# Threshold attention followed by a feed-forward block: another spacing of the weight conversion, the diagonals and the last tile

## Chip, core and metric

One core of a Trainium2 chip runs the whole program. The metric is the device time of one execution in microseconds (us). The kernel before takes 1440.85 us (median of three runs, 1439.65 to 1445.99). The profiled execution has a span of 1438.9 us from its first to its last instruction.

## The reference, cut to what matters

For 8 sequences of 576 tokens and 8 heads of 64 features:

```python
scores = (q @ k.T) / 8
thresh = max(scores, axis=-1) - tau
scores = where(scores >= thresh, scores, -1e9)
attn   = exp(scores - max(scores)); attn = attn / sum(attn)
x      = heads side by side of (attn @ v)            # 8 x 576 x 512
xn     = (x - mean(x)) / sqrt(var(x) + 1e-6) * g_ln
out    = x + relu(xn @ w_ch1) @ w_ch2                # 512 -> 2048 -> 512
```

Everything is float32, but the two weight matrices arrive as float64 and are turned into float32 on the chip, by integer operations on their words.

## The kernel before, in words

**Slots.** Attention runs in 72 slots, nine for each sequence: four pairs of heads times two halves of the queries, and one slot (the fifth) for the last 64 queries of all four pairs. Each slot has on TensorE (PE) the scores (`scores`, L384), then on VectorE (DVE) the row maxima (`neg`, L398), on ScalarE (ACT) the exponentials (L409), and on VectorE again the threshold with the row sums (`weights`, L416, and the reciprocal, L420). The scores of a slot go into the PSUM banks of the slot before, so they wait for that slot's L416. Then the weights have to be turned. In the first nine slots TensorE does it: `turn_weights` multiplies each of four blocks by a diagonal matrix that holds 1/sum (`diag`, made by ScalarE from the identity, L427), into a PSUM tile `tp`, which ScalarE copies to `em` (L462); a fifth tile `tr` takes the rest. From slot 9 on GpSimd (POOL) divides (L429), VectorE transposes blocks of 32 (L494), and the result goes by DMA to DRAM (`scr`, L500) and back (`em`, L509). A slot later TensorE multiplies by the values (`values_of`, L538).

**Feed-forward groups.** There are 16 groups of 288 tokens. For each, TensorE forms the mean (`mean_of`), VectorE subtracts it (`centre`, `xc`, L579), and `ffn_steps` issues 16 first products of four (`p1`, L100, then ReLU by ScalarE, L649) and four second products of sixteen (`p2`, L100). After the second `p1`, ScalarE squares `xc` (L653) and GpSimd adds the squares (L655); at the ninth, TensorE forms the variance (`var`), and VectorE takes the inverse root (`root`, L620 to L628) in three portions. Each finished `p2` is multiplied by that root (`add_to_x`, L596, VectorE), added to x (L597, GpSimd), transposed (L602, VectorE) and sent out (L609, four DMAs). Mean, `tp`, `tr`, `p1`, `var` and `p2` share the two PSUM buffers of the tag "ff": a tile can only begin when the operation that empties one of the two has been done.

**What sets the order.** It is written by hand, with no scheduler. A slot has four quarters; the main loop at the end of the function calls `scores`, `exponentials`, `weights` and so on, and between them `second_part(n, i)` issues as many feed-forward products as a budget gives: the products that are left of a group, spread over the quarters up to `ready(g + 1)`, with the shares `ROOM`. The call `at_quarter` puts work off to a quarter of the next slot, and the lists `aside` and `stores` hold work for the next gap. Every engine works off its instructions in the order of these calls.

**Weight conversion.** The class `Weights` converts 32 chunks (16 of each matrix) of 128 x 512. `fetch` issues the DMA of a raw chunk into a free piece of memory (rooms that belong to tiles which are not in use yet: `w2_sb`, `hidden`, `et`, `x_room`, `stage`); the table in `__init__` says up to which chunk each room may be used. A `tick` moves up to four chunks by a step each: `begin` (VectorE L263 and L267, ScalarE L271 and L275), `carry` (GpSimd L281), `mask` (VectorE L290, three ticks later) and, for the first matrix only, `end` (ScalarE L303). Slots 0 to 2 have two ticks, slots 3 to 5 three, and all from slot 6 on six. A `p1` or `p2` is issued only when its chunks have been ended in the order of the calls.

Of the kernel before, what the change touches and what calls it, by code (L numbers as in the profile page):

```python
# [18 lines left out]
def kernel(  # L19
# [31 lines left out]
    nc = tc.nc  # L51
# [114 lines left out]
    class Weights:  # L166
# [13 lines left out]
        def __init__(self):  # L180
            self.chunks = [
                (w1_sb[i][:, c : c + WC], w_ch1[i * 128 : (i + 1) * 128, c : c + WC], i)
                for c in range(0, DF, WC)
                for i in range(NK)
            ] + [
                (
                    w2_sb[:, m, d : d + 4].rearrange("p d c -> p (d c)"),
                    w_ch2[d * 128 : (d + 4) * 128, m * 128 : (m + 1) * 128].rearrange(
                        "(d p) c -> p d c", p=128
                    ),  # L190
                    None,
                )
                for m in range(NK)
                for d in range(0, ND, 4)
            ]
            self.n1 = NK * (DF // WC)
            self.fetched = self.begun = self.carried = self.masked = self.ended = 0
            self.raw, self.made, self.due, self.ticks = {}, {}, [], 2
            flat = lambda t: t.rearrange("p a b -> p (a b)")

            x_room = ffn.tile([128, NK, TOK], F32, tag="x", bufs=3, name="x_room")
            stage = consts.tile([128, 8, WC], F32, name="stage")
            et = att.tile([128, NB, 128], F32, tag="et", bufs=1, name="et0")

            n1 = self.n1
            self.free = []
            for t, n, before in (  # L210
                (w2_sb.rearrange("p m d c -> p (m d) c"), ND // 2, lambda p: n1 + 2 * p),
                (hidden, 4, lambda p: 10),
                (et, 2, lambda p: 2 * n1),
                (x_room, 1, lambda p: 2 * n1),
                (stage, 4, lambda p: 2 * n1),
            ):
                for p in range(n):
                    self.free.append((before(p), -1, flat(t)[:, p * 2 * WC : (p + 1) * 2 * WC]))
# [192 lines left out]
    def weights(es, thr, divide):  # L411


        den = small.tile([128, 4], F32, tag="den", name="den")
        for i in range(4):
            nc.vector.scalar_tensor_tensor(  # L416
                out=es[:, i], in0=blocks[i], scalar=thr[:, i : i + 1], in1=es[:, i],
                op0=ALU.is_ge, op1=ALU.mult, accum_out=den[:, i : i + 1],
            )
        nc.vector.reciprocal(den, den)  # L420
        diags = []
        for i in range(4):
            if not divide:
                if i % 2 == 0:
                    two = ffn.tile([128, TOK], F32, tag="o", bufs=6, name="diag")
                diags.append(two[:, i % 2 * 128 : i % 2 * 128 + 128])
                nc.scalar.mul(diags[i], ident, den[:, i : i + 1])  # L427
                continue
            nc.gpsimd.tensor_scalar(  # L429
                out=es[:, i], in0=es[:, i], scalar1=den[:, i : i + 1], scalar2=1.0,  # L430
                op0=ALU.mult, op1=ALU.mult,
            )
        return diags


# [7 lines left out]
    def turn_weights(s, es, diags):  # L443


        em, er = turned_tiles(s)
        for i in range(4):
            if i == 2:
                yield
            tp = ps_ff.tile([128, J, 128], F32, tag="ff", name="tp")  # L450
            for c in range(J):
                product(
                    tp[:, c], lhsT=es[:, i, c * 128 : (c + 1) * 128], rhs=diags[i],
                    start=True, stop=True,
                )
            if s == HP:
                nc.scalar.copy(
                    em[:, :, :, 32 * i : 32 * i + 32], tp.rearrange("p c (a x) -> p c a x", a=4)
                )
            else:  # L460
                h, j = divmod(i, 2)
                nc.scalar.copy(  # L462
                    em[:, :, 2 * j : 2 * j + 2, 64 * h : 64 * h + 64],
                    tp.rearrange("p c (a x) -> p c a x", a=2),
                )
        tr = ps_ff.tile([64, 4, 128], F32, tag="ff", name="tr")
        for i in range(4):
            nc.tensor.matmul(  # L468
                tr[:, i], lhsT=es[:, i, J * 128 :], rhs=diags[i], start=True, stop=True
            )  # L470
        if s == HP:
            nc.scalar.copy(
                er[:64].rearrange("p a (u x) -> p u a x", u=HP),
                tr.rearrange("p u (a x) -> p u a x", a=4),
            )
        else:
            nc.scalar.copy(
                er[:64].rearrange("p a (h x) -> p h a x", h=2),
                tr.rearrange("p (h j) (a x) -> p h (j a) x", h=2, a=2),
            )  # L480
        yield em, er
# [106 lines left out]
    def run_all(calls):  # L588
        now = calls[:]
        calls.clear()  # L590
        for fn in now:
            fn()

    def add_to_x(g, m, p2, rb):
        o = ffn.tile([128, TOK], F32, tag="o", bufs=6, name="o")
        nc.vector.tensor_mul(o, p2, rb)  # L596
        nc.gpsimd.tensor_tensor(out=o, in0=o, in1=groups[g][:, m], op=ALU.add)  # L597
        aside.append(lambda: store(g, m, o))

    def store(g, m, o):  # L600
# [4 lines left out]
    def send(g, m, ot):  # L605
        b, t = divmod(g, 2)
        for i in range(4):
            f = m * 128 + 32 * i
            nc.sync.dma_start(  # L609
                out=out[b, t * TOK : (t + 1) * TOK, f : f + 32].rearrange(  # L610
                    "(n r) c -> r n c", r=32
                ),
                in_=ot[32 * i : 32 * i + 32].rearrange("p (n c) -> p n c", c=32),
            )
# [17 lines left out]
    def ffn_steps(g):  # L632
# [5 lines left out]
        for d in range(ND):  # L638
            while conversion.ended < 4 * (d // 4 + 1):
                yield 0  # L640
            p1 = ps_ff.tile([128, TOK], F32, tag="ff", name="p1")
            for c in range(NK):
                product(
                    p1, lhsT=w1_sb[c][:, d * 128 : (d + 1) * 128], rhs=xc[:, c],
                    start=(c == 0), stop=(c == NK - 1),
                )
                if c < NK - 1:
                    yield 1
            nc.scalar.activation(hidden[:, d], p1, func=AF.Relu)  # L649
            yield 2  # L650
            if d == 1:
                sq = ffn.tile([128, NK, TOK], F32, tag="sq", bufs=1, name="sq")
                nc.scalar.activation(sq, xc, func=AF.Square)  # L653
                for c in range(1, NK):
                    nc.gpsimd.tensor_tensor(out=sq[:, 0], in0=sq[:, 0], in1=sq[:, c], op=ALU.add)  # L655
            if d == 8:
                var = ps_ff.tile([128, TOK], F32, tag="ff", name="var")
                product(var, lhsT=avg_sb, rhs=sq[:, 0], start=True, stop=True)
                rb = ffn.tile([128, TOK], F32, tag="rb", bufs=2, name="rb")
                nc.scalar.activation(sq[:, 1], var, func=AF.Identity, bias=eps_sb)  # L660
                aside.append(lambda: root(rb, sq[:, 1], sq[:, 2]))
                yield 1
# [19 lines left out]
    ROOM = (0.6, 1.0, 1.25, 0.35)  # L682
    STEPS = 1 + NK * ND * 2
    queue = []
    issued = 0
    owed = 0.0
    later_calls = {}

# [7 lines left out]
    def ready(g):  # L696

        if g < 2:
            return (24, 42)[g]
        b, t = divmod(g, 2)  # L700
        return QUARTERS * (b * SLOTS + (HP, 2 * HP)[t] + 2) + (2, 4)[t]

    def second_part(n, i):

        nonlocal issued, owed
        if not queue:
            return
        at = QUARTERS * n + i
# [40 lines left out]
    load_v(1)  # L749
    for n in range(NS):  # L750
        b, s = divmod(n, SLOTS)
        ticks = (1, 3, 4)[: 2 + n // 3] if n < 6 else range(1, 7)

        def tick(i):
            if i in ticks:
# [20 lines left out]
        second_part(n, 1)  # L776
        tick(2)
        blocks_go = by_blocks(b * HP)
        diags = weights(es, thr, blocks_go)
        run_all(aside)  # L780
        run_all(stores)
        tick(3)
        run(n, 2)
        second_part(n, 2)
        tick(4)
        box = []
        if blocks_go:
            scr = turn_blocks(s, es)
            at_quarter(n + 1, 0, lambda s=s, scr=scr, box=box: box.append(fetch(s, scr)))
        else:  # L790
            made = turn_weights(s, es, diags)
            at_quarter(n + 1, -1, next, made)
            at_quarter(
                n + 1, 0 if s <= HP else -1, lambda made=made, box=box: box.append(next(made))
            )
        at_quarter(
            n + 1, 1 if b == 0 and s <= HP else 3,
            lambda b=b, s=s, box=box: values_of(b, s, box[0]),
# [51 lines left out]
```

## Time and profile before

| What | Value |
|---|---|
| Time, median of three | 1440.85 us |
| Span of the profiled execution | 1438.9 us |
| TensorE busy | 1389.7 us (97%) |
| VectorE busy | 870.5 us (60%) |
| ScalarE busy | 421.9 us (29%) |
| GpSimd busy | 439.5 us (31%) |
| All `p1` products (L100, p<-xc) | 517.5 us |
| All `p2` products (L100, p<-hidden) | 513.6 us |
| Mean granted clock of TensorE | 0.995 |

The share of busy time is a mean over the whole span. Seen in windows of 10 us it differs much: TensorE is busy for 8.4 of 10 us from 50 to 60 us and for 6.6 from 60 to 70, and from 240 to 420 us it has no gap to speak of. So what the change can do has to be read from the first 215 us and from the last few.

The slots of the first part can be told by the maxima of VectorE (L398), two operations for each slot. In the profiled execution those of slots 3 to 11 begin at 50.63, 65.17, 79.68, 93.11, 123.20, 149.08, 168.44, 194.94 and 215.39 us.

### The profile page before, as it was taken

How to read it: one execution, taken by the hardware profiler on the slowest of the kernel's cores; microseconds unless marked ns; L12 is line 12 of the kernel's file. 1: busy time of each engine (PE TensorE's matmuls, PEld its weight loads, DVE VectorE, ACT ScalarE, POOL GpSimd, SP SyncE). 2: the span in 40 equal slices, each digit the busy share in tenths (PEclk: the TensorE clock that was granted, in tenths of full speed). 3: DMA queues.
4: the chain of work that ended last, by engine and by line, in shares of the span. 5: the costliest groups of instructions: out<-in, count | busy, mean ns of one | idle time of the engine just before them, and what ended most of it. 6: DMA issues, size and time to landing. Idle time of an engine off the chain costs nothing.

```text
span 1438.9 us, 29660 instructions
## 1 busy us (share of the span) xinstructions
PE 1389.7 (97%) x12168; PEld 852.3 (59%) x12168; DVE 870.5 (60%) x1492; ACT 421.9 (29%) x818; POOL 439.5 (31%) x681
## 2 busy tenths in 40 slices
PE   4879999999999999999999999999999999999998
PEld 3655665655556555655556555665556555565664
DVE  5998857556665666556665565656665666656111
ACT  3886513132222313132221312213132222213020
POOL 2344342333323233232322233232332323222100
PEclk8999999999999999999999999999999999999999
DMA  9622456558855587557855577556775578455301
GB/s 226 173 70 82 90 130 164 163 136 172 178 145 144 142 182 169 143 134 170 188 152 145 147 151 175 142 145 146 173 177 146 131 170 185 135 145 136 79 6 17
DMA packets 466840, 205.12 MB, mean 143 GB/s; under 512 B 275024, under 2 KB 428368, under 8 KB 466704
## 3 DMA queue, kind: packets, MB, share of 16 engines
q1 hardware_dynamic: 461936, 202.64, 57.9%
q8 instruction: 95, 1.56, 0.5%
q10 hardware_dynamic: 4736, 0.59, 0.4%
q14 instruction: 41, 0.34, 0.1%
q0 software_dynamic: 32, 0.00, 0.0%
HBM read 119.41 MB, written 83.76 MB: 141 GB/s over the span
## 4 chain that ended last, share of the span: by engine, by line
PE 89%; DVE 4%; ACT 2%; SPq 1%; issue 1%; DMA 1%; POOL 0%; POOLq 0%; ACTq 0%; DVEq 0%
PE p L100 67%; PE sc L538 10%; PE sc L384 10%; PE tp L100 1%; DVE e L416 1%; DMA em<-scr 1%; DVE neg L398 1%; SPq L500 1%; PE mean L100 0%; PE var L100 0%; DVE w L263 0%; ACT e L409 0%; PE tr L468 0%; SPq L129 0%; SPq L133 0%
## 5 line engine op out<-in xcount | busy, mean ns | idle before, releaser
L100 PE MATMUL p<-xc,w 128*64 128x288 f32 x4096 | 517.5, 408 | 6.5 <-ACT hidden L649 4.5
L100 PE MATMUL p<-hidden,w 128*64 128x288 f32 x4096 | 513.6, 407 | 0.0
L100 PEld LDWEIGHTS p<-xc,w 128*64 128x64 f32 x4096 | 291.8, 137 | 216.3 <-ACT hidden L649 14.4
L100 PEld LDWEIGHTS p<-hidden,w 128*64 128x64 f32 x4096 | 295.3, 137 | 199.1 <-issue 9.3
L398 DVE TENSOR_REDUCE neg<-sc 128x2 f32<-128x1152 f32 x144 | 188.8, 1352 | 250.1 <-PE sc L384 250.1
L409 ACT ACTIVATE e<-sc,neg 128x576 f32<-128x576 f32 x288 | 194.4, 742 | 261.7 <-DVE neg L398 256.2
L429 POOL TENSOR_SCALAR e<-e,den 128x576 f32<-128x576 f32 x252 | 188.5, 766 | 240.5 <-DVE den L420 240.4
L416 DVE SCALAR_TENSOR_TENSOR e<-sc,thr,e 128x576 f32<-128x576 f32 x288 | 219.1, 811 | 27.8 <-ACT e L409 27.8
L494 DVE STREAM_TRANSPOSE et<-e 128x1152 f32<-128x1152 f32 x112 | 153.6, 1375 | 78.3 <-POOL e L429 58.2
L649 ACT ACTIVATE hidden<-p 128x288 f32<-128x288 f32 x256 | 105.7, 413 | 284.5 <-PE p L100 282.9
L384 PE MATMUL sc<-kT,qT 64*128 64x384 f32 (+3 forms) x1024 | 150.2, 424 | 20.0 <-DVE qT L344 10.1
L402 POOL TENSOR_SCALAR thr<-neg,low_sb 128x2 f32<-128x2 f32 x144 | 41.9, 291 | 352.2 <-DVE neg L398 343.3
L384 PEld LDWEIGHTS sc<-kT,qT 64*128 64x128 f32 x1024 | 94.2, 191 | 77.2 <-issue 27.5
L538 PE MATMUL sc<-em,v_in 128*64 128x256 f32 (+1 forms) x1408 | 131.4, 330 | 2.1 <-DMA em<-scr 2.1
L555 ACT COPY x<-sc 128x256 f32<-128x256 f32 x60 | 22.3, 372 | 316.9 <-PE sc L538 291.9
L538 PEld LDWEIGHTS sc<-em,v_in 128*64 128x64 f32 x1408 | 86.2, 138 | 41.6 <-issue 2.9
L597 POOL TENSOR_TENSOR o<-o,x 128x288 f32<-128x288 f32 x64 | 51.4, 804 | 151.4 <-DVE o L596 151.4
L596 DVE TENSOR_TENSOR o<-p,rb 128x288 f32<-128x288 f32 x64 | 28.1, 439 | 103.5 <-PE p L100 103.0
L564 POOL TENSOR_TENSOR sum<-sum,x 128x256 f32<-128x256 f32 (+1 forms) x64 | 32.7, 511 | 71.8 <-ACT x L555 69.3
L655 POOL TENSOR_TENSOR sq<-sq 128x288 f32<-128x288 f32 x48 | 38.8, 808 | 42.1 <-ACT sq L653 39.6
L564 POOL TENSOR_TENSOR sum<-x 128x256 f32<-128x256 f32 (+1 forms) x32 | 16.7, 523 | 98.8 <-ACT x L555 57.3
L538 PE MATMUL sc<-rest,v_rest 128*64 128x256 f32 (+1 forms) x352 | 44.4, 329 | 0.0
(130 smaller groups left out, 715.0 us busy)
## 6 DMA issues: line engine op xcount, KB each, us to landing
scr<-et SPq DMA_DIRECT2D x252, 288.0 KB, 4.8
em<-scr SPq DMA_DIRECT2D x63, 1024.0 KB, 5.9
out_dram<-ot SPq DMA_DIRECT2D x256, 36.0 KB, 4.2
q_in<-in_q_dram SPq DMA_DIRECT2D x124, 72.0 KB, 3.4
k_in<-in_k_dram SPq DMA_DIRECT2D x120, 72.0 KB, 2.6
v_in<-in_v_dram SPq DMA_DIRECT2D x64, 128.0 KB, 4.5
rest<-scr SPq DMA_DIRECT2D x63, 128.0 KB, 5.9
w<-in_moe_w_ch_dram SPq DMA_DIRECT2D x10, 512.0 KB, 5.9
```

What stands on the lines that cost most here:

```text
L100: nc.tensor.matmul(out[r], lhsT=lhsT[:, r], rhs=rhs, **flags)
L384: nc.tensor.matmul(sc[h][64 * i : 64 * i + 64 if s == HP else 128, at : at + n], lhsT=ql[r] if s == HP else qT[r, half, j * 128 : (j + 1) ...
L398: nc.vector.tensor_reduce(out=neg[:, i], in_=pairs[h], axis=AXL.X, op=ALU.max, negate=True,)
L402: nc.gpsimd.tensor_scalar(out=thr[:, i], in0=neg[:, i], scalar1=-1.0, scalar2=low_sb, op0=ALU.mult, op1=ALU.add,)
L409: nc.scalar.activation(es[:, i], blocks[i], func=AF.Exp, bias=neg[:, i : i + 1])
L416: nc.vector.scalar_tensor_tensor(out=es[:, i], in0=blocks[i], scalar=thr[:, i : i + 1], in1=es[:, i], op0=ALU.is_ge, op1=ALU.mult, accum_o ...
L429: nc.gpsimd.tensor_scalar(out=es[:, i], in0=es[:, i], scalar1=den[:, i : i + 1], scalar2=1.0, op0=ALU.mult, op1=ALU.mult,)
L494: nc.vector.transpose(et[:, :, 64 * h : 64 * h + 64].rearrange("p n (j c) -> p j n c", j=2), es[:, 2 * h : 2 * h + 2].rearrange("p j (n c) ...
L538: nc.tensor.matmul(dst[64 * h : 64 * h + 64], lhsT=vt[:, c, h, :] if c < J else vr[:, h, :], rhs=pick(em[:, c] if c < J else er, hp, h), s ...
L564: nc.gpsimd.tensor_tensor(out=sums[g][:, cols], in0=x[:, 0, cols] if c == 1 else sums[g][:, cols], in1=x[:, c, cols], op=ALU.add,)
L597: nc.gpsimd.tensor_tensor(out=o, in0=o, in1=groups[g][:, m], op=ALU.add)
L649: nc.scalar.activation(hidden[:, d], p1, func=AF.Relu)
```

## The change

It has these parts, none of which alters what is computed:

- **Ticks**: slots 3 to 5 have two conversion ticks instead of three. So 12 of the 32 chunks have been begun before slot 6, where there were 15.
- **Rooms**: pieces of `hidden` are given up from chunk 8 on (before: 10), those of `et` from chunk 28 on (before: not until the end). In slots 5 to 8 there is one more call of `fetch(2)`.
- **Diagonals**: they become a function of their own. In slots 5 to 7 ScalarE makes them after the second quarter's products and not right after the reciprocal.
- **Ninth slot** (slot 8): its four blocks are turned one a quarter (before the exponentials, then in the quarters 0, 1 and 2 of slot 9), not two and two before and after the maxima.
- **Variance**: it isn't formed in the first quarter of a slot, unless it is the last chance.
- **Second group**: it begins at quarter 43 and not at 42, so that its mean is formed in the third quarter of slot 10.
- **Last tile** of the last group: VectorE and not GpSimd adds x, and two of its four DMAs are issued from ScalarE.

```diff
-                (hidden, 4, lambda p: 10),
-                (et, 2, lambda p: 2 * n1),
+                (hidden, 4, lambda p: 8),
+                (et, 2, lambda p: 28),
...
         nc.vector.reciprocal(den, den)
-        diags = []
-        for i in range(4):
-            if not divide:
...
+        for i in range(4 if divide else 0):
...
+    def diagonals(den):
...
         for i in range(4):
-            if i == 2:
+            if i:
                 yield
...
-        nc.gpsimd.tensor_tensor(out=o, in0=o, in1=groups[g][:, m], op=ALU.add)
+        last = (g, m) == (NG - 1, NK - 1)
+        engine = nc.vector if last else nc.gpsimd
+        engine.tensor_tensor(out=o, in0=o, in1=groups[g][:, m], op=ALU.add)
...
-            nc.sync.dma_start(
+            (nc.scalar if last and i % 2 else nc.sync).dma_start(
...
-            if d == 8:
+            if d >= 8 and rb is None and (part or d == ND - 1):
...
-            return (24, 42)[g]
+            return (24, 43)[g]
...
-        ticks = (1, 3, 4)[: 2 + n // 3] if n < 6 else range(1, 7)
+        ticks = (1, 3) if n < 6 else range(1, 7)
...
-        diags = weights(es, thr, blocks_go)
+        den = weights(es, thr, blocks_go)
+        if n <= HP or n == 2 * HP:
+            diags = diagonals(den)
         run_all(aside)
         run_all(stores)
+        if HP < n < SLOTS:
+            conversion.fetch(2)
         tick(3)
         run(n, 2)
         second_part(n, 2)
+        if HP < n < 2 * HP:
+            diags = diagonals(den)
         tick(4)
...
-            at_quarter(n + 1, -1, next, made)
-            at_quarter(
-                n + 1, 0 if s <= HP else -1, lambda made=made, box=box: box.append(next(made))
-            )
+            for i, at in enumerate(
+                (-1, -1, 0, 0) if s <= HP else (-1, -1, -1, -1) if s < 2 * HP else (-1, 0, 1, 2)
+            ):
```

## The prediction, made before the changed kernel was run

> **What bounds the kernel now.** I read the page's busy shares and its forty slices first.
>
> ```profile
> PE 1389.7 (97%) x12168; PEld 852.3 (59%) x12168; DVE 870.5 (60%) x1492; ACT 421.9 (29%) x818; POOL 439.5 (31%) x681
> PE   4879999999999999999999999999999999999998
> DVE  5998857556665666556665565656665666656111
> ```
>
> TensorE bounds the span as a whole; its work stays the same, so only its gaps can be won: 16 us before 20 us (first loads), some 23 us from 20 to 240, 3 from there to 1380, 6 at the end. The windows (columns: busy time and count of PE, PEld, DVE, ACT, POOL, then clock and DMA) show who bounds the gappy stage:
>
> ```profile
> 60.00:70.00 10.00, 6.59 (x97) 5.41 (x91) 9.90 (x11) 7.68 (x15) 5.44 (x5) 1.00 0.13 40
> 70.00:80.00 10.00, 7.64 (x80) 5.56 (x78) 9.90 (x17) 9.15 (x19) 3.98 (x4) 1.00 0.16 56
> 80.00:90.00 10.00, 7.43 (x124) 5.97 (x120) 9.90 (x18) 7.94 (x17) 4.37 (x7) 1.00 0.33 105
> 110.00:120.00 10.00, 8.92 (x62) 5.20 (x64) 9.25 (x9) 5.90 (x13) 6.00 (x5) 0.83 0.37 122
> ```
>
> VectorE is full there. The waits of TensorE up to 215 us agree: scores wait for L416, and turned blocks for ScalarE, whose exponentials wait for the maxima.
>
> ```profile
> PE sc L384 <- DVE e L416: 11.0, 9, 7.3
> PE tp L100 <- ACT em L462: 5.3, 5, 1.8
> PE p L100 <- ACT hidden L649: 3.8, 2, 2.8
> PE p L100 <- DVE o L596: 0.7, 1, 0.7
> ```
>
> Then the timelines. On VectorE, what the third tick of slot 4 costs:
>
> ```profile
> 76.92 0.69 DVE L290 SCALAR_TENSOR_TENSOR w<-w 128x512 f32<-128x512 f32 x1
> 77.52 1.52 DVE L263 TENSOR_SCALAR w<-x_room 128x512 uint32<-128x512 uint32 x1
> 79.07 0.69 DVE L267 SCALAR_TENSOR_TENSOR w<-x_room,w 128x512 uint32<-128x512 uint32 x1
> ```
>
> On TensorE, the second group's mean in slot 10 and the wait after it:
>
> ```profile
> 197.24 0.66 PE L100 MATMUL mean<-sum,avg_sb 128*64 128x288 f32 x4
> 204.95 1.43 PE L100 MATMUL p<-xc,w 128*64 128x288 f32 x10 [0.74 <-DVE o L596]
> ```
>
> **The skill.** "TensorE: Matmul & The Clock Gate", Part 1, says that an idle window of about 3.4 us halves the clock until TensorE has been busy as long. The trace agrees in kind: after 7.26 us of idling the scores at 21.17 took 5.68 us, elsewhere 2.21; after 2.76 us at 108.3 the next 36 records took 1.9 us more than at full clock. "SBUF — State Buffer", section "SBUF: two separate sides", says that VectorE with two SBUF inputs or in a two-port mode and GpSimd lock each other out for a whole instruction. Agrees: L267 takes 0.69 us, and 1.68 to 1.83 where L281 runs. So one tick costs VectorE 1.7 us, or 2.8 with the lock.
>
> **The change, step by step.** Times are those of the trace before; the order of the changed program's instructions gives the rest.
>
> 1. Slots 3 and 4 lose the tick shown: 62.41 to 65.17 and 76.92 to 79.68, 2.76 us each. VectorE remains the bound (14.5 - 2.76 = 11.75 us a slot; ScalarE needs 10.3, TensorE 9). Slot 5 loses 1.79, but `xc` is next on VectorE and needs the mean, which TensorE can end only 2.75 us after L416; this leaves 0.76. The maxima of slot 6 start 6.3 us earlier, at 86.8. The turned blocks gain 6.7, since `tp` and `mean` get their buffer earlier.
> 2. Slot 6. TensorE: 28 products instead of 32 (0.49 us each), and a tick less ahead of L649 because the diagonals stand behind it; it reaches the next scores at about 109.4 instead of 120.9. But VectorE has the same six ticks. Its chain there (26.45 us, with 5.1 of idling that hang on ScalarE and GpSimd and move along) ends at 112.9. The 3.65 us that it waited for scores before are gone: from here VectorE is behind TensorE.
> 3. Slot 7: VectorE has the same instructions, all back to back, 25.9 us. Slot 8: 12.3 us up to the reciprocal, then three full ticks and a mask, 3 x 2.2 + 0.6 = 7.3 (between 5.7 and 8.7 by the lock), where before 7.0 stood. Maxima of slot 9 at 158.4, 10.0 earlier.
> 4. Slot 9: maxima and transposes 4.6, `o` 0.4, a tick and a mask 2.9, L416 and reciprocal 3.2, to the end of L494 5.6 (as from 181.4 to 187.0): 175.0.
> 5. What is new: three chunks later means that the last two chunks are fetched at the end of slot 9. Their DMAs stand on the queue behind the four of `scr`, and VectorE's L263 for them stands ahead of the maxima of slot 10.
>
> ```profile
> 187.13 3.80 SPq L500 DMA_DIRECT2D scr<-et  x4
> 159.05 0.43 SPq L243 DMA_DIRECT2D w<-in_moe_w_ch_dram  x1
> ```
>
> So 3.9 us for issuing `scr`, 0.5 for the first chunk, and 5.5 for the second to land (3.4 without other traffic, 5.9 the page's median; up to 8 behind 1.2 MB of `scr`). Then L263 and L267 1.1 and L602 0.45: 11.5 in all, against 7 to 14. Maxima of slot 10 at 186.5, while TensorE ends those scores at about 181. Queued behind: maxima, exponentials, L416, and the `o` of the third `p2`.
> 6. Now the mean comes after 14 products of slot 10, and the "ff" buffers are held by the third and the fourth `p2`. It waits for that third `o`, which stands behind L416 of slot 10: 8.8 us after the maxima began (9.5 before, less `ot` and `xc`, plus a mask), 195.3. TensorE is there at 187.8, and idles about 7.5 us.
> 7. Sum: before, the mean began at 197.24 with 119 products done; now at 195.3 with 118. So 195.3 + 0.5 - 197.2 = -1.4; the later wait of 0.74 for `o` goes, as `xc` and `o` are ready: -2.2. After such a gap the clock is slow: +1.9 (up to 3.4).
> 8. The end:
>
> ```profile
> 1433.34 0.79 POOL L597 TENSOR_TENSOR o<-o,x 128x288 f32<-128x288 f32 x1 [7.03 <-DVE o L596]
> 1434.16 0.48 DVE L602 STREAM_TRANSPOSE ot<-o 128x288 f32<-128x288 f32 x1 [0.97 <-POOL o L597]
> ```
>
> The 0.97 us become about 0.5 on VectorE, without a crossing; and four issues of 0.46 on one queue become two on each of two, 0.7 less: -1.2 (0.8 to 1.6).
>
> At nothing: later diagonals in slots 5 to 7 (the blocks they feed come after the next scores), the blocks of slot 8 one a quarter (0.69 us each of waiting saved or not, while VectorE sets the end of this stage), the later variance (it changes places with products), the rooms, and later pacing, because TensorE is full from slot 11 on.
>
> Together -2.2 + 1.9 - 1.2 = -1.5: 1439.4.
>
> **Rivals.** *The fetch is hidden*: the raw chunks land early, or VectorE is less late by some 6 us, so that the maxima of slot 10 begin at about 181. Then the mean begins at 189.7, 2 us of waiting and no slow clock: 189.7 + 0.5 - 197.2 - 0.7 = -7.7, with the end -8.9: 1432. For it: chunks landed in 3.4 to 4.2 us when the queue was free, and VectorE has slack of 10 us in slots 9 and 10. Against it: the queue's order puts `scr` first, and `scr` needs the end of L494. *Slower*: ticks locked as in the worst stretch (+1.4 in slot 8, +1 in slot 9), the second chunk landing after 8 us (+2.5), and the slow clock 3.4 instead of 1.9 (+1.5): -1.5 + 6.4, about 1446. For it: 1.2 MB of `scr` ahead on all 16 engines; against: windows of 344 GB/s occur.
>
> **How the numbers follow.** The bound by VectorE and the queue: 0.60. Hidden: 0.25. Slower: 0.15. The likeliest gives 1439.4. Its own unknowns are about 3 us to either side; the range is drawn from just under the hidden case to just short of the slower one, 1430.5 to 1445.5. Faster by over 0.5% means under 1433.6: most of the hidden case and a little of the first, 0.27. Slower by over 0.5% means over 1448: the upper part of the slower case, 0.06. Else 0.67.
>
> **What would show it.** Maxima of slots 4, 5 and 6 near 62.4, 74 and 87, those of slot 9 near 158; on VectorE a wait of several us for `stage` at the end of slot 9; the mean waiting for `o` L596 for some 7 us with a lower clock after it; L597 gone from the end. The prediction is wrong if the mean waits under 3 us (then nearly all of the early gain stays), or if VectorE isn't behind TensorE in slots 7 to 9.

## The result, and the profile after

The changed kernel takes 1446.86 us (median of six runs, 1445.69 to 1448.00) against 1440.96 for the kernel before in the same comparison: a ratio of 1.0036, interval 1.0020 to 1.0051. It is slower by 5 to 6 us, where 1.5 us less was forecast, and the time lies 1.4 us above the upper end of the range (1445.5). The profiled spans are 1438.9 and 1445.1 us.

From the page of the changed kernel, the busy shares and TensorE's row of the slices:

```profile
PE 1391.4 (96%) x12168; PEld 853.0 (59%) x12168; DVE 871.8 (60%) x1493; ACT 421.7 (29%) x818; POOL 438.4 (30%) x680
PE   4889879999999999999999999999999999999998
```

A slice is 36 us. The third is better than it was (8 for 7), the fifth and sixth (145 to 217 us) are worse (8 and 7 for 9). The windows of the changed kernel say the same more sharply (busy time and count of PE, PEld, DVE, ACT, POOL; then granted clock, DMA share, GB/s):

```profile
60.00:70.00 10.00, 8.85 (x112) 6.78 (x103) 9.93 (x15) 9.02 (x17) 3.80 (x4) 1.00 0.06 20
...
110.00:120.00 10.00, 10.00 (x122) 7.61 (x120) 9.90 (x13) 7.62 (x14) 4.04 (x4) 1.00 0.23 66
...
180.00:190.00 10.00, 2.51 (x17) 1.61 (x14) 2.06 (x3) 2.45 (x5) 1.02 (x2) 0.67 0.96 253
```

From 60 to 70 us TensorE is busy for 8.85 us where it was 6.59, and from 110 to 120 it is full at the full clock. From 180 to 190 us all five engines are nearly empty, 2.51 us at most, while the DMA engines are busy for 96% of the time. Most of them wait for the same transfers. These are TensorE's waits up to 215 us in the changed kernel (us in total, times, longest):

```profile
PE sc L384 <- ACT x L558: 10.2, 3, 7.5
...
PE mean L100 <- DVE o L599: 2.0, 1, 2.0
PE tp L100 <- ACT em L465: 1.4, 2, 0.7
```

The turned blocks wait 1.4 us where they waited 5.3. New are 10.2 us in which scores wait for L558, the copy by which ScalarE empties the values' product out of the banks that the scores need: 7.5 us of it in slot 10 and 2.5 in slot 9. The three timelines of the changed kernel around 180 us show the order. SyncE's queue (SPq), then ScalarE, then VectorE:

```profile
176.37 3.81 SPq L503 DMA_DIRECT2D scr<-et  x4
180.28 3.07 SPq L243 DMA_DIRECT2D stage<-in_moe_w_ch_dram  x2
```

```profile
187.33 0.67 ACT L271 ACTIVATE stage<-stage 128x512 int32<-128x512 uint32 x1 [13.77 <-DMA stage<-in_moe_w_ch_dram]
...
188.46 0.38 ACT L558 COPY x<-sc 128x256 f32<-128x256 f32 x1
```

```profile
187.33 0.43 DVE L263 TENSOR_SCALAR x_room<-stage 128x512 uint32<-128x512 uint32 x1 [10.64 <-DMA stage<-in_moe_w_ch_dram]
...
190.04 1.66 DVE L267 SCALAR_TENSOR_TENSOR stage<-stage 128x512 uint32<-128x512 uint32 x1
...
193.20 2.62 DVE L398 TENSOR_REDUCE neg<-sc 128x2 f32<-128x1152 f32 x2 [1.12 <-PE sc L384]
```

The four DMAs of `scr` go out at 176.37, once the transposes (L497) end; only then, at 180.28, go the last two chunks. The first lands at 187.33, 7.0 us later. Two engines stand in front of it: VectorE with L263, and ScalarE with L271, behind which the copy L558 waits although its data has long been there. TensorE in the same stretch:

```profile
188.89 4.21 PE L384 MATMUL sc<-kT,qT 64*128 64x384 f32 x16 [7.49 <-ACT x L558]
...
202.38 0.71 PE L100 MATMUL mean<-sum,avg_sb 128*64 128x288 f32 x4 [2.02 <-DVE o L599]
202.89 5.05 PE L100 MATMUL p<-hidden,w 128*64 128x288 f32 x40
```

The scores wait 7.49 us and then take 4.21 us, nearly twice the 2.21 that they take elsewhere in this trace; the mean waits another 2.02 us for `o` and comes at 202.38 us, where it stood at 197.24 before. The chain of waits of the changed kernel goes through the same pieces (start, us, what):

```profile
180.28 7.03 DMA stage<-in_moe_w_ch_dram
...
188.59 0.27 ACT x L558
188.89 4.26 PE sc L384 x16
```

The last tile, on VectorE in the changed kernel, has lost the crossing to GpSimd:

```profile
1440.08 0.46 DVE L599 TENSOR_TENSOR o<-p,rb 128x288 f32<-128x288 f32 x1 [5.91 <-PE p L100]
1440.57 0.46 DVE L602 TENSOR_TENSOR o<-o,x 128x288 f32<-128x288 f32 x1
```

From the start of that L599 to the end of the span it is 1445.1 - 1440.08 = 5.0 us; before, L596 began at 1432.73, 6.2 us ahead of the end.

Against the trace of before, the maxima (L398) of slots 4 to 11 moved so:

| Slot | Before | After | Difference |
|---|---|---|---|
| 4 | 65.17 | 62.33 | -2.8 |
| 5 | 79.68 | 74.06 | -5.6 |
| 6 | 93.11 | 86.89 | -6.2 |
| 7 | 123.20 | 112.92 | -10.3 |
| 8 | 149.08 | 138.86 | -10.2 |
| 9 | 168.44 | 160.28 | -8.2 |
| 10 | 194.94 | 193.20 | -1.7 |
| 11 | 215.39 | 214.28 | -1.1 |

So up to slot 8 ten microseconds are won. Of these 2.1 are given back up to slot 9 and 6.4 more between slots 9 and 10. The last row still shows 1.1 us in favour of the changed kernel, and yet its span is 6.2 us longer: it has done fewer products by then, since the second group's mean is formed 5.1 us later. What lies behind the mean is in the last experiment.

### The profile page after: what moved, and what is told of

It is laid out like the page before. It is cut to its first block, busy times and chain, and to the rows that moved or that the text cites. A ratio compares the mean times of both kernels' runs of the same rounds, so it can differ in the third digit from the quotient of the medians.

```text
span 1445.1 us, 29661 instructions
## 1 busy us (share of the span) xinstructions
PE 1391.4 (96%) x12168; PEld 853.0 (59%) x12168; DVE 871.8 (60%) x1493; ACT 421.7 (29%) x818; POOL 438.4 (30%) x680
## 4 chain that ended last, share of the span: by engine, by line
PE 84%; DVE 7%; ACT 2%; DMA 2%; issue 1%; SPq 1%; POOL 1%; POOLq 0%; ACTq 0%; DVEq 0%
PE p L100 63%; PE sc L384 10%; PE sc L541 10%; DVE e L416 2%; DVE neg L398 1%; DMA em<-scr 1%; PE tp L100 1%; ACT e L409 1%; SPq L503 1%; PE mean L100 1%; DMA stage<-in_moe_w_ch_dram 0%; POOL e L422 0%; DMA scr<-et 0%; DVE w L290 0%; DVE et L497 0%
## 5 line engine op out<-in xcount | busy, mean ns | idle before, releaser
L398 DVE TENSOR_REDUCE neg<-sc 128x2 f32<-128x1152 f32 x144 | 188.8, 1352 | 255.4 <-PE sc L384 255.4
L416 DVE SCALAR_TENSOR_TENSOR e<-sc,thr,e 128x576 f32<-128x576 f32 x288 | 219.2, 811 | 20.0 <-ACT e L409 20.0
L497 DVE STREAM_TRANSPOSE et<-e 128x1152 f32<-128x1152 f32 x112 | 153.3, 1374 | 77.4 <-POOL e L422 59.7
L655 ACT ACTIVATE hidden<-p 128x288 f32<-128x288 f32 x256 | 105.8, 414 | 275.5 <-PE p L100 273.9
L384 PE MATMUL sc<-kT,qT 64*128 64x384 f32 (+3 forms) x1024 | 153.8, 433 | 30.2 <-ACT x L558 10.2
L558 ACT COPY x<-sc 128x256 f32<-128x256 f32 x60 | 22.3, 372 | 318.0 <-PE sc L541 294.8
L599 DVE TENSOR_TENSOR o<-p,rb 128x288 f32<-128x288 f32 x64 | 28.0, 438 | 99.9 <-PE p L100 99.4
```

The lines of the kernel that those rows point to most:

```text
L384: nc.tensor.matmul(sc[h][64 * i : 64 * i + 64 if s == HP else 128, at : at + n], lhsT=ql[r] if s == HP else qT[r, half, j * 128 : (j + 1) ...
L398: nc.vector.tensor_reduce(out=neg[:, i], in_=pairs[h], axis=AXL.X, op=ALU.max, negate=True,)
L416: nc.vector.scalar_tensor_tensor(out=es[:, i], in0=blocks[i], scalar=thr[:, i : i + 1], in1=es[:, i], op0=ALU.is_ge, op1=ALU.mult, accum_o ...
L497: nc.vector.transpose(et[:, :, 64 * h : 64 * h + 64].rearrange("p n (j c) -> p j n c", j=2), es[:, 2 * h : 2 * h + 2].rearrange("p j (n c) ...
```

## The experiments

**Theory A**: the place of the last two fetches behind `scr` gives the gain back. It has two routes: A1, over VectorE (L263, then maxima, row sums, `o`, mean), as the prediction had it; and A2, over ScalarE (L271, then the copy L558, then the scores), which it had not seen. **Rivals**: the fewer early ticks leave too much conversion for later; or the second group begins too late, a quarter behind where it stood; or one of the edits that were costed at nothing isn't free. Ratios are against the kernel before in the same comparison, since its own median moved between 1440.46 and 1442.1 us from one to the next. The traces are of one execution each, and these differ by up to 1.3 us already at the maxima of slot 3 (50.11 to 51.43 us), ahead of what the experiments' edits move. So a difference of that size between the times of two traces says something only where a wait of the same size stands beside it.

| Run | Time, us | Ratio, interval |
|---|---|---|
| changed kernel | 1446.86 | 1.0036 (1.0020 to 1.0051) |
| fetch ahead | 1438.71 | 0.9982 (0.9973 to 0.9990) |
| tick behind the copy | 1446.69 | 1.0043 (1.0029 to 1.0057) |
| ticks back | 1448.62 | 1.0045 (1.0029 to 1.0060) |
| fetch ahead, second group at 42 | 1440.24 | 1.0000 (0.9990 to 1.0009) |
| before, last tile alone | 1440.01 | 0.9985 (0.9978 to 0.9993) |
| fetch ahead, copy ahead in slot 8 | 1439.85 | 0.9987 (0.9980 to 0.9994) |
| fetch ahead, three edits undone | 1440.99 | 0.9994 (0.9984 to 1.0004) |
| fetch ahead, `o` ahead | 1434.07 | 0.9945 (0.9930 to 0.9960) |
| the same again | 1435.00 | 0.9967 (0.9954 to 0.9979) |
| fetch ahead, copy and `o` ahead | 1437.52 | 0.9972 (0.9956 to 0.9987) |
| `o` ahead alone | 1443.94 | 1.0024 (1.0010 to 1.0038) |
| fetch and `o` ahead, variance later | 1431.17 | 0.9935 (0.9923 to 0.9947) |

### Fetching ahead of the transposed weights

```diff
         box = []
+        if n == SLOTS:
+            conversion.fetch(2)
         if blocks_go:
             scr = turn_blocks(s, es)
```

> The changed kernel, with one more fetch(2) in slot 9 ahead of turn_blocks, so that the DMAs of the last two weight chunks stand on the queue before the four of scr and not behind them. Nothing else moves. Theory A (the wait is for these DMAs: ScalarE's L271 waits for them, the copy of x, L558, stands behind L271, and the scores of slot 10 wait for x): the chunks are issued at about 173.6 us and land by 179, the wait of the scores (7.5 us) and the slow clock after it (2.4 us) go, the wait of the mean for o stays at about 2 us: about 1437 us, 10 less than the changed kernel and 4 less than the kernel before. Theory B (VectorE is late anyway after slots 7 to 9, and what is gained at the scores is lost again at the mean): 3 less than the changed kernel, 1444.

Measured: 1438.71 us (21 runs), ratio 0.9982, some 0.0054 or 8 us below the changed kernel, and below the kernel before too. Its trace, VectorE and TensorE:

```profile
178.35 0.45 DVE L263 TENSOR_SCALAR x_room<-stage 128x512 uint32<-128x512 uint32 x1 [1.02 <-DMA stage<-in_moe_w_ch_dram]
```

```profile
182.13 2.21 PE L384 MATMUL sc<-kT,qT 64*128 64x384 f32 x16
...
193.63 0.71 PE L100 MATMUL mean<-sum,avg_sb 128*64 128x288 f32 x4 [2.35 <-DVE o L599]
```

The chunks are issued at 174.25 instead of 180.28, which is 6.0 us, and the first is there 4.1 us later instead of 7.0, which is another 2.9: L263 begins 9.0 us earlier. The scores of slot 10 wait for nothing and take 2.21 us again, the maxima come at 184.44, and the mean comes 8.75 us earlier. The place in the queue is the cause of the late mean; theory A holds. The mean still waits 2.35 us for `o`.

### The tick behind the copy: only the route over ScalarE taken away

```diff
-        tick(5)
+        if n != SLOTS:
+            tick(5)
         run(n, 3)
+        if n == SLOTS:
+            tick(5)
```

> The changed kernel, with the fifth tick of slot 9 after the values of slot 8, so that ScalarE copies x before it waits for the last chunks (L558 before L271). The DMAs stay behind scr, and VectorE's L263 for them stays ahead of the maxima of slot 10. Theory A1 (two chains hang on the late DMAs, and the one over VectorE is only a little shorter): the scores of slot 10 begin at about 181.4 and don't wait, but the maxima begin at about 192 instead of 193.2 and the mean waits some 10 us instead of 2: 1445 to 1446, hardly less than the changed kernel. Theory A2 (only the copy of x matters): the 7.5 us and the slow clock go, 1437.

Measured: 1446.69 us, ratio 1.0043: nothing won. ScalarE now copies at 181.32 us and TensorE's scores come at 182.17 without a wait, but (TensorE of this run):

```profile
182.17 2.21 PE L384 MATMUL sc<-kT,qT 64*128 64x384 f32 x16
...
201.75 1.23 PE L100 MATMUL mean<-sum,avg_sb 128*64 128x288 f32 x4 [10.44 <-DVE o L599]
202.74 6.56 PE L100 MATMUL p<-hidden,w 128*64 128x288 f32 x40
```

The wait has only moved: 7.49 and 2.02 us in two places have become 10.44 in one, and the mean stands at 201.75 instead of 202.38. The route over VectorE (L263 waits 11.28 us here, maxima at 192.62) is by itself nearly as long. So A1 is right as the prediction had it, and A2 is a second route beside it that is about a microsecond longer: it cost 1.1 us of waiting at the maxima in the changed kernel and has gone here (0.6 us at the mean between the two traces). The low clock has moved with the wait: the mean and the 40 products behind it take 7.4 us from start to start (201.75 to 209.12) where they took 5.4 in the changed kernel, so what was won at the scores is lost here. The profiled execution was the slowest of this kernel's four (1450.20 us; the others 1446.24 to 1446.77).

### The early ticks back

```diff
-        ticks = (1, 3) if n < 6 else range(1, 7)
+        ticks = (1, 3, 4)[: 2 + n // 3] if n < 6 else range(1, 7)
```

> The changed kernel, with the ticks of slots 3 to 5 as before (three in each). By the order of its instructions one chunk instead of two is still fetched behind scr in slot 9. Theory A (the loss comes from the chunks behind scr): the early gain of 6 us is given back and a shorter wait at slot 10 remains, 5 us and a slow clock of 2, so it isn't faster than the changed kernel: 1445 to 1448. Theory C (it is the fewer ticks that push the conversion into slot 10; with them back the loss is gone): about 1439.7, the kernel before less the 1.2 us of the last tile.

Measured: 1448.62 us, ratio 1.0045. With the ticks of before, the slots are late again (maxima of slot 6 at 92.73 us, of slot 8 at 144.18), but one chunk is still fetched behind `scr`, and L263 waits 8.73 us for it. TensorE of this run:

```profile
187.93 4.21 PE L384 MATMUL sc<-kT,qT 64*128 64x384 f32 x16 [4.74 <-ACT x L558]
```

The mean comes at 201.12, 1.3 us earlier than in the changed kernel, and the time is the same within the intervals (the profiled execution was this kernel's fastest, 1443.91 us). The missing ticks aren't what costs; one chunk behind `scr` does nearly the same harm as two. With one chunk it is the route over ScalarE that sets the end: VectorE is ready at 187.9, and its maxima wait 4.30 us for the late scores. The rival falls.

### Fetching ahead, and the second group a quarter earlier

```diff
-            return (24, 43)[g]
+            return (24, 42)[g]
```

> As e1_fetch_ahead, and the second group at quarter 42 as in the kernel before, so that its mean comes after the first products of slot 10, when a buffer is free, and not while two second products hold both. Theory A: the remaining wait of 2 us of the mean for o goes, about 1435. If mean and o aren't the wait that is left: as e1_fetch_ahead, 1437.

Measured: 1440.24 us, ratio 1.0000, against 0.9982 with the quarter left at 43; this was expected to gain and didn't. The mean is earlier (191.74 without a wait), but the next second product waits for the mask of its chunk, which stands on VectorE behind the row sums (TensorE of this run):

```profile
191.74 0.66 PE L100 MATMUL mean<-sum,avg_sb 128*64 128x288 f32 x4
...
196.54 6.91 PE L100 MATMUL p<-hidden,w 128*64 128x288 f32 x32 [3.66 <-DVE w L290]
```

A wait of 2.35 us is replaced by one of 3.66: with the last chunks' masks so late, the later quarter is the better one up to here. (The profiled execution, 1444.73 us, was the slowest of this kernel's twelve.) The second group's later beginning isn't what holds the mean; what it does to the steady part is in the last experiment.

### The last tile alone

The kernel before, with only the edit of the last tile (as in the change's diff: `engine` for the addition, `nc.scalar` for two of the DMAs).

> The kernel before with the edit of the last tile alone: VectorE adds x to the very last tile and two of its four DMAs are issued from ScalarE. If the end was costed rightly (step 8 of the prediction): 1.15 us shorter from the last product to the end of the span, nothing else moved, 1439.7 to 1440 us against 1441, ratio 0.9992. If part of the loss of the changed kernel came from the end: 1441 or more.

Measured: 1440.01 us against 1442.1, ratio 0.9985 (0.9978 to 0.9993). The expected 0.9992 lies inside this interval. In its trace L596 of the last tile begins at 1433.37 and the span ends at 1438.4: 5.0 us, as in the changed kernel. This part brings what it was costed at, and none of the loss comes from it.

### Fetching ahead, and the copy of slot 8 ahead of its tick

```diff
-        if n <= HP or n == 2 * HP:
+        if n <= HP:
             diags = diagonals(den)
...
-        if HP < n < 2 * HP:
+        if HP < n <= 2 * HP:
             diags = diagonals(den)
...
-        tick(5)
+        if n != SLOTS - 1:
+            tick(5)
         run(n, 3)
+        if n == SLOTS - 1:
+            tick(5)
```

> The changed kernel with the last two chunks fetched ahead of the transposed weights (as in the run that fetched ahead), and in slot 8 the copy of the values' product (L558) ahead of the fifth tick, and the diagonals of slot 8 after the third quarter's products. It takes away most of TensorE's wait of 2.5 us for that copy at 157 us and the low clock after it (3.55 us for the scores instead of 2.21). If VectorE alone sets the end of slots 8 to 10, its maxima of slot 9 still start at about 160 and those of slot 10 at 184: at most 0.5 us shorter than fetching ahead, 1438.2 to 1438.7. If TensorE's gap is on the path: 2.5 to 3.9 us shorter, about 1435.5.

Measured: 1439.85 us, ratio 0.9987, no better than fetching ahead alone (0.9982). TensorE's scores of slot 9 now wait 0.30 us instead of 2.54 and take 2.21 instead of 3.55, and yet the maxima of slot 10 stand at 184.26 (184.44 when only fetching ahead) and the mean at 193.45 (193.63): 0.2 us, and nothing if one counts from the maxima of slot 3. What TensorE gained it loses to a later wait of 2.62 us for a turned block's copy (L465). That copy stands on ScalarE behind exponentials, and these wait 2.83 us for VectorE's maxima of slot 9. So far VectorE sets the pace, as the prediction said. In slot 10 it no longer does (VectorE of this run):

```profile
184.26 2.62 DVE L398 TENSOR_REDUCE neg<-sc 128x2 f32<-128x1152 f32 x2 [4.25 <-PE sc L384]
```

With the fetch ahead the maxima of slot 10 wait for TensorE's scores, 4.25 us here and 3.00 with the fetch alone.

### Fetching ahead, with the three edits undone that were costed at nothing

```diff
-        if n <= HP or n == 2 * HP:
+        if n <= 2 * HP:
             diags = diagonals(den)
...
-        if HP < n < 2 * HP:
-            diags = diagonals(den)
...
-                (-1, -1, 0, 0) if s <= HP else (-1, -1, -1, -1) if s < 2 * HP else (-1, 0, 1, 2)
+                (-1, -1, 0, 0) if s <= HP else (-1, -1, -1, -1)
...
-            if d >= 8 and rb is None and (part or d == ND - 1):
+            if d == 8:
```

> The changed kernel with the last two chunks fetched ahead, and with the three edits that were costed at nothing undone: the diagonals right after the reciprocal in slots 5 to 7, the blocks of slot 8 turned ahead of the maxima of slot 9, the variance at the ninth first product. If they cost and bring nothing: 1438.7, within 1 us either way. If one of them carries part of the loss, it is 2 us or more shorter; if the later diagonals are what lets TensorE reach the scores of slots 6 to 8 early, 2 us or more longer.

Measured: 1440.99 us, ratio 0.9994 against 0.9982: 1.7 us longer, with intervals that overlap. VectorE's maxima of slot 7 in this run:

```profile
114.33 2.62 DVE L398 TENSOR_REDUCE neg<-sc 128x2 f32<-128x1152 f32 x2 [1.62 <-PE sc L384]
```

They wait 1.62 us for the scores, where in the changed kernel they come at 112.92 without a wait; slot 10 stands at 186.84, where fetching ahead had 184.44. In slot 6 TensorE waits 2.79 us for a ReLU (L655) that stands on ScalarE behind the diagonals, where it waited 1.6 with the diagonals behind it. So the diagonals' place in slot 6 is worth one to two microseconds in these traces, as step 2 of the prediction said, though its list of edits at nothing had them. The three edits together don't cost, and may bring one or two microseconds.

### Fetching ahead, and `o` ahead of the row sums in slot 10

```diff
+        if n == SLOTS + 1:
+            run_all(aside)
         den = weights(es, thr, blocks_go)
```

> The changed kernel with the last two chunks fetched ahead, and in slot 10 the product of the third second-product tile with the root (o, L599) ahead of the row sums (L416) on VectorE. Fetching ahead left TensorE waiting 2.35 us at the mean of the second group for this o, which stood behind four L416. If that order is what still holds the mean: the mean starts at about 191.3 without a wait and not at 193.6, TensorE is full from there, 1436.4. If the next wait takes its place (xc behind L416, as the mask did when the second group began a quarter earlier): 1438 to 1439.

> The kernel with the last two chunks fetched ahead and o (L599) ahead of the row sums in slot 10, once more, beside a variant with one further edit. The first time it took 0.9945 of the time before, of which the traces explain about 0.9965 (2.35 us of wait at the mean beside the gain of fetching ahead). If the traces tell all of it: 0.996 to 0.997 this time. If the whole of it holds: 0.9945.

Measured: 1434.07 us, ratio 0.9945 (0.9930 to 0.9960), and again 1435.00, ratio 0.9967 (0.9954 to 0.9979). VectorE and TensorE of the first:

```profile
187.86 0.44 DVE L599 TENSOR_TENSOR o<-p,rb 128x288 f32<-128x288 f32 x1
188.22 0.80 DVE L416 SCALAR_TENSOR_TENSOR e<-sc,thr,e 128x576 f32<-128x576 f32 x1
```

```profile
189.08 0.66 PE L100 MATMUL mean<-sum,avg_sb 128*64 128x288 f32 x4
```

The mean waits for nothing. From the maxima of slot 10 to those of slot 11 it is 18.54 us instead of 21.08, which is 2.5 us won, as the traces said. The first measurement is lower by 2 to 3 us more. Its trace is 1.3 us ahead already at slots 3 and 8 (138.44 against 139.73), where the two kernels are the same, and another 0.7 at slot 10, since the scores of slot 9 happened to run at the full clock (2.21 us against 3.55 with the fetch alone). The second measurement, 0.9967 where 0.9965 is explained, bears out the traces. `o` behind four L416 is a real wait, in series with the fetch.

### All three ahead

The edits of the three kernels before (fetch, copy of slot 8, `o`) together.

> The changed kernel with all three: the last two chunks fetched ahead, in slot 8 the copy L558 ahead of the fifth tick (diagonals after the third quarter's products), and in slot 10 o (L599) ahead of the row sums. Both remaining gaps of some 2.5 us on TensorE up to slot 10 are taken away, and with them the stretches of low clock that follow such gaps in some executions. If these stretches matter: maxima of slot 9 at 159.5, mean at 189 to 190, 1433 to 1434, and closer together than with o ahead alone (1434.07). If VectorE's chain from slot 8 to 10 is all that counts: the same 1434 as with o ahead alone. If the copy ahead moves a wait to the turned blocks (2.6 us there in the run with the copy ahead): 1435 to 1436.

Measured: 1437.52 us, ratio 0.9972: no better than without the copy, with the 2.62 us at the turned blocks again and a clock of 0.83 from 160 to 170 us behind them. The expectation that taking away both gaps would help is missed; the third of its cases came, and somewhat more. The profiled execution was one of the three short ones of eight (1434.71 us), so its trace doesn't show what the longer ones lost.

### `o` ahead alone

> The changed kernel with o (L599) ahead of the row sums in slot 10 and nothing else; the last two chunks stay behind the transposed weights. In the changed kernel's trace the mean waited 2.02 us for this o, after scores that had waited 7.49 us for the copy behind the chunk. If the two waits are in series, as the trace says: 2 to 2.5 us less, about 1444.5, and the wait at the scores stays at 7 to 7.5 us. If the o was the main cause and the fetch only a witness: 1438 or less.

Measured: 1443.94 us, ratio 1.0024 (the changed kernel: 1.0036). In its trace the scores wait 7.43 us for L558, as before, and the mean none. So the two waits are in series, the fetch is the larger, and `o` is worth about 2 us. Its mean is at 201.04 instead of 202.38.

### The variance still later

```diff
-            if d >= 8 and rb is None and (part or d == ND - 1):
+            if d >= 8 and rb is None and (part > 1 or d == ND - 1):
```

on top of the fetch and `o` ahead. The reason is in TensorE's waits from 215 us on. The kernel before:

```profile
PE sc L538 <- DMA em<-scr: 2.1, 2, 1.3
PE p L100 <- ACT hidden L649: 0.7, 1, 0.7
```

and the changed kernel:

```profile
PE p L100 <- ACT hidden L655: 3.5, 5, 0.7
PE sc L541 <- DMA em<-scr: 1.4, 2, 1.0
```

With the small ones (0.3 for `xc` in both, 0.4 for `et` in the second), 3.1 us have become 5.6. Where the five waits of 0.70 stand, TensorE of the changed kernel shows (one of them):

```profile
399.68 2.16 PE L100 MATMUL p<-xc,w 128*64 128x288 f32 x16
401.67 0.66 PE L100 MATMUL var<-sq,avg_sb 128*64 128x288 f32 x4
403.03 1.19 PE L100 MATMUL p<-xc,w 128*64 128x288 f32 x8 [0.70 <-ACT hidden L655]
```

After the scores comes one `p1` (16 products), then the variance, which takes the other of the two "ff" buffers, and so the next `p1` needs the first one's ReLU, which stands between exponentials on ScalarE. In the kernel before the variance of this group came after two `p1`, without a wait.

Two parts of the change could have brought this: the second group's later start, which shifts all later products against the slots, and the variance's own edit. The runs above part them to some degree. Fetching ahead with the three edits undone (variance at the ninth `p1` as before, second group at 43), and fetching ahead with the second group at 42 (variance as changed):

```profile
PE p L100 <- ACT hidden L655: 3.5, 5, 0.7
```

```profile
PE p L100 <- ACT hidden L655: 4.9, 7, 0.7
```

The later start is enough for the five waits without the variance's edit, and setting the start back with that edit in place doesn't take them away. No run has the start at 42 and the variance as before, with the rest of the change.

> The same kernel, and the variance isn't formed in the second quarter of a slot either. After 215 us the changed kernel's TensorE waits five times 0.70 us for the ReLU L655 where the kernel before waits once, mostly where the variance comes after a single first product behind the scores. If its place there is the cause: at most one or two of these waits are left, 2.1 to 2.8 us less than the kernel beside it. If any place in a slot gives such a wait: no difference, within 0.7 us. If the later root delays the first o of a group: 1 us or more longer.

Measured: 1431.17 us, ratio 0.9935 (0.9923 to 0.9947), against 0.9967 of the kernel beside it: 0.0032, some 4 us, more than the 2.1 to 2.8 expected. Its waits from 215 us on, but for 0.3 us for `xc`:

```profile
PE sc L541 <- DVE sq L633: 1.4, 2, 0.8
```

All five for the ReLU are gone; two others of together 1.4 us have come, which the profile puts down to the root. That is 4.5 us of waiting in the kernel beside it and 1.7 here, 2.8 less. The rest is before the mean, which comes 1.4 us earlier. Of this 0.6 stands already at slot 3, where the edit changes nothing; the other 0.8, with scores of slot 9 that neither wait nor run slow here, wasn't separated. This kernel is faster than the one before (by some 9 us) and the changed one (by some 14).

## Why the prediction was wrong

From mean to end both kernels do the same work but for one product, so the span's difference can be summed term by term:

| Term | Predicted | Measured |
|---|---|---|
| second group's mean, one product less | -1.4 | 202.38 + 0.5 - 197.24 = +5.6 |
| later wait for `o` gone | -0.7 | -0.7 |
| low clock after the mean | +1.9 | 0 |
| waits from 215 us on | 0 | +2.5 |
| the end | -1.2 | -1.15 |
| sum | -1.5 | +6.2 (spans: +6.2) |

Two terms failed: the time of the mean, which is step 5, and the later pacing, which was put at nothing.

**Steps 1 to 3 were right.** Maxima of slots 4 to 8 were forecast at 62.4, 74, 86.8, 112.9 and near 139, and came within 0.1 us or so. TensorE was at the scores of slot 7 at 109.42 us (forecast 109.4), and VectorE was behind it in slots 7 and 8. One sum of step 2 doesn't come out as written: 86.8 + 26.45 is 113.25 and not 112.9; the chain took 26.0 us, so that its 112.9 came true in part by luck. Slot 9 was 1.9 us later than forecast: 1.2 us of ticks, inside the bounds given, and 0.7 us of waiting for scores. There VectorE wasn't behind, because the copy L558 stood behind ScalarE's ticks of slot 8 and TensorE's scores waited 2.52 us for it.

**Step 5 is the one that failed, in its sizes.** The mechanism stands, as the runs with the fetch ahead and with the tick behind the copy show: the last fetches are behind `scr`, and VectorE holds the maxima, the row sums and `o` behind them. But from the end of the transposes (176.34) to the maxima of slot 10 it was 16.9 us, not 11.5, and outside the 7 to 14 given. Four terms: the second chunk was used 8.8 us after the issue began and not 6.0 (+2.8), because each issue took 1.5 us and each landing 7.0 to 7.1 behind `scr`; its L263 and L267 took 2.6 us and not 1.1 (+1.5), with GpSimd's L281 of the first chunk running beside them (189.68, 1.47 us), a length that step 3 allowed for ticks but step 5 didn't; the maxima waited 1.1 us for scores; and `o` came 0.4 us later. With slot 9's 1.3 at the end of the transposes this is 7.1 us, the whole distance from 195.3 to 202.38. The last-but-one of these terms is what was overlooked, not mis-sized: "TensorE ends those scores at about 181" left out that ScalarE's L271 waits for the same chunk with the copy L558 behind it. (Even with the fetch ahead and no wait those scores end at 184.3.) The Trainium skill ("TensorE: Matmul & The Clock Gate", Part 1, on engine queue depths) says that ScalarE and VectorE are strictly first in, first out; the copy at 188.46, directly behind L275, agrees. The run that freed the copy shows that this alone cost about a microsecond, since the other route was nearly as long.

**Step 6** was right in that the mean waits behind `o`, and wrong on where the idling lies: 7.49 us at the scores and 2.02 at the mean, not 7.5 at the mean. By the letter its own sign of being wrong came true ("if the mean waits under 3 us"), but what the sign stood for did not: the early gain was gone all the same, since TensorE had idled at the scores.

**Step 7.** The low clock came at the scores (2.0 us longer), not after the mean, where 40 products took 5.05 us, the full rate (0.126 us each; 36 took 4.54 in the kernel before). So the 1.9 us weren't to be added at the mean; the 1.1 us that the maxima waited are what came of it, since scores of 2.21 us would have ended at about 191.1 (an estimate), when VectorE wasn't ready before 192.1. The price itself was about right: where the idling did lie at the mean, with the tick behind the copy, the mean and its 40 products took 2.0 us more. The reading it was taken from is a little high: the 36 records behind the wait of 2.76 us took 5.9 us (111.08 to 116.97), and at the full clock the same would take 4.2 (an estimate from 20 products at 194.77 and 16 records of `values_of` at 161.93 in the same trace), which makes 1.7 more.

**At nothing.** "Later pacing, because TensorE is full from slot 11 on" failed too: TensorE's waits from 215 us on grew by 2.5 us, +2.8 by four more waits for the ReLU and -0.3 by the others, which differ from trace to trace. TensorE was full, but where the groups' products fall against the slots decides whether the variance meets a single `p1`. With the variance formed later these waits vanish.

**Step 8** was right: 1.15 us in the trace, and the run with this edit alone agrees.

Of the rivals, "slower" (about 1446, with 0.15) is nearest to what happened, and its number is nearer than its reasons. Of its terms the late second chunk came (+2.8 for 2.5) and half of the locked ticks (1.2 us in slot 8, none in slot 9); the slow clock of 3.4 us after the mean did not. The second chunk's own two operations and the later pacing, which it didn't name, made up for that by chance. "The fetch is hidden" needed the maxima of slot 10 at about 181; even ahead of `scr` they came at 184.44, so this case lay further off than it looked.

What stays open: why the steady part waits seven times with the second group back at 42, where the kernel before waited once; why the time of the kernel with the early ticks back isn't lower although its mean is 1.3 us earlier, and how much of the last variant's gain before the mean is its edit's.

## What to carry to other kernels

When a change moves work later, look up every engine that uses what arrives late, and what stands behind each use on an engine that works in order: here the same chunk held VectorE's and ScalarE's queues, and the two routes were about a microsecond apart, so that freeing one brought nothing. A DMA that is needed soon goes ahead of the issues that wait for late data; moving two issues by a few lines was worth 8 us. And a change of pacing isn't free on a full engine: list the waits of the steady part before and after, since five waits of 0.7 us are invisible in a busy share.

## What the runs showed of the hardware

- A chunk of 512 KB landed 4.1 us (the first) and 5.1 us (the second) after its issue ahead of `scr`, and 7.0 to 7.1 us behind the 1.2 MB of `scr`; the two issues took 0.95 us there and 3.07 us here.
- The low clock came after shorter gaps than expected, and not every time. After a wait of 2.51 to 2.55 us the scores of slot 9 took 3.52 to 3.80 us in five traces and 2.21 in a sixth, and the kernel of the sixth (fetch and `o` ahead, first time) is also one of the five (the same again). "TensorE: Matmul & The Clock Gate", Part 1, gives an idle window of about 3.4 us that runs freely; that the same gap is punished or not agrees with a free-running window, that 2.5 us can be enough doesn't agree with its length, and the measurement decides.
